# Moving two gate computations from the head of a query stage into the middle of the down stage before it

## The chip, the cores and the metric

The kernel runs on one core of one Trainium2 chip. The time is device microseconds of one execution, as the median over several runs. A core has engines that run side by side, each with its own in-order instruction queue: TensorE (PE, with its weight loads as PEld), VectorE (DVE), ScalarE (ACT), GpSimd (POOL) and SyncE (SP), which here issues most DMAs.

## The reference

Two branches work on the same input x (2048 rows of 1024 bf16 values) and are mixed by a gate, one number for each row:

```python
g = sigmoid((x * gate_w).sum(-1, keepdims=True))
a = attention(x, wqkv) @ wo      # 32 heads of 32, window of 8 keys at distance 2
b = (gelu(x @ w_gate) * (x @ w_up)) @ w_down     # 3584 wide
out = g * a + (1 - g) * b
```

Each query looks at the keys 0, 2, ... 14 rows back; keys ahead of the first row are masked.

## The kernel before, in words

The 2048 rows are cut into four **chunks** of 512. Chunks 0 and 1 form the first pair, 2 and 3 the second. For each pair the program makes queries, keys and values (`qkv_pair`, `first_pair`), then the GLU branch (`ffn`), and then for each chunk the **down stage** (`down`, `down_rest`), which multiplies the GLU result by w_down and the attention result by wo and adds both in the same PSUM banks. So TensorE's order is: query, key and value products of pair 0, `ffn` 0, down 0, query, key and value products of pair 1, some blocks of `ffn` 1, down 1, the rest of `ffn` 1, down 2, down 3.

All large products of a pair are made in a scheme of seven products where eight would be plain (Strassen's, in Winograd's form). It needs sums and differences of the operands, made on VectorE:

- **forms of x**: four operations in `x_forms` (L516, L518, L520, L521). L520 overwrites part of chunk 2's x, so it must come after the gate of that chunk has read x.
- **forms of the weights**: for the queries, keys and values eight operations on L709 for each (four forms in two halves, `qkv_forms`).
- **forms of the GLU result** for the down stage (L1266, `down_forms`).

The seven products of a down stage are numbered m = 0 to 6, each made for two halves g = 0, 1. Product 0 is in `begin`; products 1 to 6 run in `down_rest` in the order (1,0), (1,1), (2,0) ... (6,1). Each is 18 matmuls of 128x512 on line L1305: 14 with the GLU result (tile hT) and four with the attention result (tile qo). What each leaves: m = 2 a scaled copy m5d in the buffers with tag `m5`, m = 3 a copy u2d in those with tag `u2`; m = 4 adds its bank and m5d into an output tile (L1377 before the change), m = 5 its bank and u2d (L1383), m = 1 and m = 6 are scaled out by ScalarE (L1346). The output tiles are stored by GpSimd (L1338). In this text the "fifth product" is m = 4 and the "sixth" is m = 5.

The query products of the second pair begin in `first_pair` with line L592: for t = 0 to 3, a product over the first half of the contraction (four matmuls, and a seeding copy L604 by ScalarE), then the second half (L592 again, copied out by L625). Then come the products of the forms on L772, at first with tf (forms of x), and after the queries the rest in `qkv_pair`, where a bank with a product is copied or added out by L798, L808, L820, L830 and L858 (ScalarE) and by **L837** and **L847** (VectorE). A later product (T4 in `qkv_pair`) is accumulated in the bank which L837 has read, so TensorE waits for L837 there. The same part in `first_pair` is done by L657 and L667.

**The gate** of chunk c (`gate`): eight matmuls (L874) of gate_w with x into one PSUM bank, a 32x32 block transpose of it to a tile zt in SBUF by VectorE (L880), and a small copy zq of every 32nd column (L884). The bank is given back after L880. `gate_sum` later sums zq by a small matmul.

**Attention** of a chunk is VectorE work that goes on beside all stages: `scores` multiplies queries with shifted keys (L937) and adds up (L943); the sum is turned by a DMA transpose (L1006); L1014 to L1060 make the softmax; ScalarE spreads the weights (L1066); two DMA transposes of 256 KB each (**L1075**) turn them back; then L1084 multiplies with the values and L1094, L1098, L1102 add up. The first L1084 waits for both L1075.

**Who sets the order.** A planner (`Weave`) takes a number of streams (main, loads, scores, attention, forms and so on), estimates with costs that are written in the code when each next operation could start, and emits the earliest one, with a bias or a due time for some. The order in which it emits is fixed for each engine by manual dependencies. So where one step in `main` is moved, the planner may choose another order for the operations of other streams around it, on every engine. Once built, every engine's queue is in that order whatever the real times are.

Weights arrive in a **ring** of 20 slots of 256 KB (L352 for the query, key and value weights, L400 for `ffn`, L420 for down), loaded by SyncE in a fixed order; a load waits for its slot to be given back. L1075 and L1006 are issued by SyncE too and stand in the same queue. An L709 needs the loads of its weights; the first one waits for all eight loads of its matrix. Eight PSUM banks of 128x512 float32 are handed out by `bank_take`, the one that the planner thinks free the earliest first.

## Time and profile before

| what | value |
|---|---|
| median of 4 runs | 725.92 us (725.33 to 727.16) |
| the profiled execution's own time | 726.34 us |
| its span, first to last instruction | 724.6 us |
| granted TensorE clock, mean | 0.998 |
| TensorE busy in the span | 711.5 us |
| VectorE busy in the span | 610.1 us |
| first down stage (L1305), about | 250.9 to 307.8 us |
| gates of chunks 2 and 3 (L874) | 307.76 to 308.74 us |
| query products of the second pair (L592) | 308.74 to 321.1 us |
| key and value products (L772) | up to 388 us |

The profile is of one execution. Times are from the start of its span. A timeline's row has start, duration, engine, source line, operation, tiles written and read, and in brackets how long the engine was idle before it and what ended that. A row of windows has, for a stretch of time, the busy time of each engine with its instruction count, the granted TensorE clock as a share, the DMA engines' share and GB/s. Matmuls overlap, so one takes 0.379 us but they follow each other every 0.216 us. Rows of VectorE overlap a little too: an operation shown as 1.22 us lets the next one start after 1.13 to 1.14.

### The profile page before, as it was taken

To read this page: it belongs to the slowest core of one execution; us is meant where nothing else is said; L and a number is where in the kernel's file an instruction comes from. 1 tells how busy PE (TensorE), PEld (TensorE's weight loads), DVE (VectorE), ACT (ScalarE), POOL (GpSimd) and SP (SyncE) were. 2 spreads that over 40 slices of the span, in tenths; PEclk is the share of its full clock that TensorE was granted. 3 is DMA by queue.
4 is the path that set the end of the run, shared out by engine and by line. 5 is a ranking of instruction groups with operands and counts; after the bars stand their busy time and mean duration, and the time that the engine had idled before them with its cause. 6 is when DMAs were issued, how large, how long until landed. Compare 5 with 4: busy or idle time off the path is not lost.

```text
span 724.6 us, 9885 instructions
## 1 busy us (share of the span) xinstructions
PE 711.5 (98%) x3337; PEld 342.8 (47%) x3337; DVE 610.1 (84%) x862; ACT 323.8 (45%) x547; POOL 73.8 (10%) x130
## 2 busy tenths in 40 slices
PE   7999999999999999979999999999999999999997
PEld 4556544444444444446655444444444444444443
DVE  4989999999999999699779998799999997849300
ACT  3354585555585422144465413257556755310110
POOL 0021233343111000100000000100000000001000
PEclk9999999999999999999999999999999999999999
DMA  9943899996897799932468899997657755999992
GB/s 265 369 179 101 262 279 333 350 316 203 199 255 204 262 229 342 343 121 88 139 182 283 263 314 336 320 314 191 173 152 184 180 156 164 313 287 378 312 328 97
DMA packets 184179, 176.84 MB, mean 244 GB/s; under 512 B 58304, under 2 KB 140224, under 8 KB 184000
## 3 DMA queue, kind: packets, MB, share of 16 engines
q1 hardware_dynamic: 174512, 145.53, 68.4%
q0 software_dynamic: 9328, 30.42, 11.4%
q8 instruction: 26, 0.43, 0.2%
q10 hardware_dynamic: 288, 0.26, 0.1%
q14 instruction: 25, 0.20, 0.1%
HBM read 132.12 MB, written 31.46 MB: 226 GB/s over the span
## 4 chain that ended last, share of the span: by engine, by line
PE 94%; DMA 2%; DVE 2%; SPq 1%; issue 0%; ACT 0%; DVEq 0%
PE ps L1136 47%; PE ps L1305 29%; PE ps L772 18%; DMA ring<-in_A_wqkv_dram 2%; DVE ring L709 1%; PE ps L592 1%; SPq L357 1%; DMA hT<-in_A_wqkv_dram 1%; DVE zt L880 0%; SPq L428 0%; DVE tf L518 0%; DVE tf L521 0%; DVE lend L520 0%; DVE lend L837 0%; ACT ost L1346 0%
## 5 line engine op out<-in xcount | busy, mean ns | idle before, releaser
L1136 PEld LDWEIGHTS <-ring 128*128 128x128 bf16 x1568 | 153.3, 98 | 185.0 <-issue 0.5
L1136 PE MATMUL ps<-lend,ring 128*128 128x512 bf16 x896 | 212.6, 379 | 0.0
L1136 PE MATMUL ps<-tf,ring 128*128 128x512 bf16 x672 | 164.3, 379 | 0.0
L1305 PE MATMUL ps<-ring,hT 128*128 128x512 bf16 x708 | 160.6, 379 | 0.0
L1305 PEld LDWEIGHTS <-hT 128*128 128x128 bf16 x708 | 69.3, 98 | 83.5
L1084 DVE TENSOR_TENSOR xbuf<-xbuf,lend 128x2048 bf16<-128x2048 bf16 x64 | 77.6, 1218 | 14.4 <-DMA xbuf<-xbuf 14.3
L772 PEld LDWEIGHTS <-ring 128*128 128x128 bf16 x512 | 64.8, 127 | 48.7 <-issue 2.6
L937 DVE TENSOR_TENSOR xbuf<-qo,lend 128x2048 bf16<-128x2048 bf16 x64 | 77.3, 1218 | 2.7 <-ACT lend L830 2.6
L943 DVE TENSOR_TENSOR xbuf<-xbuf 128x2048 bf16<-128x2048 bf16 x56 | 68.2, 1218 | 0.2
L772 PE MATMUL ps<-tf,ring 128*128 128x512 bf16 x256 | 58.4, 379 | 2.4 <-DVE tf L516 0.9
L772 PE MATMUL ps<-lend,ring 128*128 128x512 bf16 x256 | 57.9, 379 | 0.0
L1346 ACT ACTIVATE ost<-ps,omg 128x512 bf16<-128x512 f32 x16 | 11.0, 687 | 99.6 <-PE ps L1305 99.6
L1212 ACT ACTIVATE gl<-ps 128x512 bf16<-128x512 f32 x56 | 33.5, 598 | 47.8 <-PE ps L1136 46.6
L1168 ACT COPY ps<-ps 128x512 f32<-128x512 f32 x56 | 32.1, 573 | 50.9 <-PE ps L1136 50.6
L1305 PE MATMUL ps<-ring,qo 128*128 128x512 bf16 x192 | 49.3, 379 | 0.0
L1338 POOL DMA_DIRECT2D out_dram<-ost x24 | 13.0, 541 | 335.7 <-ACT ost L1346 248.0
L505 POOL DMA_DIRECT2D fforms<-ring x56 | 30.8, 550 | 144.3 <-DVE ring L496 138.3
L1185 DVE TENSOR_TENSOR hT<-hT,gl 128x1024 bf16<-128x1024 bf16 x56 | 38.4, 686 | 8.3 <-ACT hT L1178 8.2
L1224 DVE TENSOR_TENSOR u<-ps,u 128x512 f32<-128x512 f32 x56 | 38.4, 686 | 3.2 <-PE ps L1136 2.3
L1228 ACT ACTIVATE gl<-u 128x512 bf16<-128x512 f32 x56 | 35.4, 633 | 9.9 <-DVE u L1224 9.5
L1220 ACT COPY u<-ps 128x512 f32<-128x512 f32 x56 | 32.8, 586 | 14.6 <-PE ps L1136 14.6
L1094 DVE TENSOR_TENSOR xbuf<-xbuf 128x2048 bf16<-128x2048 bf16 x32 | 39.0, 1219 | 0.1
(120 smaller groups left out, 671.3 us busy)
## 6 DMA issues: line engine op xcount, KB each, us to landing
ring<-dforms SPq DMA_DIRECT2D x112, 256.0 KB, 4.9
ring<-in_B_w_down_dram SPq DMA_DIRECT2D x84, 256.0 KB, 5.4
ring<-in_B_w_gate_dram SPq DMA_DIRECT2D x56, 256.0 KB, 5.3
fforms<-ring POOLq DMA_DIRECT2D x56, 256.0 KB, 5.1
ring<-fforms SPq DMA_DIRECT2D x56, 256.0 KB, 4.0
ring<-in_B_w_up_dram SPq DMA_DIRECT2D x42, 256.0 KB, 4.8
ring<-in_A_wqkv_dram SPq DMA_DIRECT2D x32, 256.0 KB, 4.5
ring<-oforms SPq DMA_DIRECT2D x32, 256.0 KB, 5.4
```

Of the source, the lines that this page charges most:

```text
L772: nc.tensor.matmul(banks[bk][:], lhsT=lhsT, rhs=rhs[:, kt, :], start=(start and kt == 0), stop=(kt == KH - 1), skip_group_check=True)
L937: V(out=w3(box[t]), in0=q_b, in1=k_w, op=ALU.mult)
L943: V(out=w3(box[0]), in0=w3(box[0]), in1=w3(box[t]), op=ALU.add)
L1084: return dve(tt(n), taking(("p", t), lambda: V(out=w3(box["p", t]), in0=w3(box["ab"]), in1=v_w, op=ALU.mult)), [("qkv", c, 2, t), abo] + ( ...
L1094: V(out=p0.rearrange("p (u n) -> p u n", u=2), in0=lo, in1=hi, op=ALU.add)
L1136: nc.tensor.matmul(banks[bk][:], lhsT=wv[:, k, fl * P:(fl + 1) * P], rhs=rhs[:, k, :], start=(start and k == 0), stop=(k == KH - 1), skip_ ...
L1185: yield dve(tt(2 * SC), lambda hv=hv, gv=gv: nc.vector.tensor_tensor(out=hv, in0=hv, in1=gv, op=ALU.mult), [e, ev[f, "g1"], ev[f, "g2"]], ...
L1212: nc.scalar.activation(out=gl[f][:, r1 * SC:(r1 + 1) * SC], in_=banks[A[f]][:], func=ACT.Gelu_apprx_tanh)
L1220: nc.scalar.copy(out=u2[f][:], in_=banks[Bk[f]][:])
L1224: e = dve(tt(SC, True), lambda f=f: nc.vector.tensor_tensor(out=u2[f][:], in0=banks[Dk[f]][:], in1=u2[f][:], op=ALU.add), [o, ev[f, "u2"]])
L1228: ev[f, "g2"] = act(0.54, lambda f=f: nc.scalar.activation(out=gl[f][:, r2 * SC:(r2 + 1) * SC], in_=u2[f][:], func=ACT.Gelu_apprx_tanh), [ ...
L1305: nc.tensor.matmul(banks[bk][:], lhsT=l, rhs=wv[:, i, :], start=(start and k == 0), stop=(q == last and i == 1), skip_group_check=True)
```

## The change

`main` made the gates of chunks 2 and 3 after the first down stage, just ahead of the second pair's query products. Now `down_rest` of chunk 0 makes both just ahead of its product (5, 0), the sixth; the tile zt of those two gates comes from the buffers with tag `m5` rather than `u2`. Nothing else in the text of the program differs.

```diff
-        zt = work.tile([P, SC], F32, tag="u2", bufs=2, name="zt")
+        zt = work.tile([P, SC], F32, tag="m5" if c > 1 else "u2", bufs=2, name="zt")
...
         for m, g in steps:
+            if (m, g) == (5, 0) and c == 0:
+                yield from gate(2)
+                yield from gate(3)
...
         yield from parts[2]
         yield from halo(2)
-        yield from gate(2)
-        yield from gate(3)
         yield from qkv_pair(2, [0])
```

In the built program the lines behind the insertion are three higher, so L1377 becomes L1380 and L1383 becomes L1386. The planner also orders some other operations anew. The listing of the two built programs shows, from the fifth product on:

- VectorE before: L1377, L937, L943, L937, L1383, L943, L943, L937, L1383, L943, six L709, L520, L521, L880, L709, L884, L880, L709, L884, L1084, L1084, L1094, L1084, ...
- VectorE after: L1380, L520, L521, L880, L884, L880, L884, L937, L1386, L943, L1386, L1084, L1084, L1094, eight L709, L1084, L1098, L943, L1084, ...; and two L937 and two L943 stand just ahead of the first L837 of the key and value products.
- SyncE before: two L352, L1075, six L352, L1075, fourteen L352. After: two L352, L1075, L1075, twenty L352.
- GpSimd: the same order. ScalarE: the same kinds of operations in nearly the same order, on other banks.

## The prediction

> **What bounds the kernel now.** I read the page's first and fourth parts, then the chain in order of time, then the timelines of the stage that the change touches, from 290 to 350 us.

> ```profile
> PE 711.5 (98%) x3337; PEld 342.8 (47%) x3337; DVE 610.1 (84%) x862; ACT 323.8 (45%) x547; POOL 73.8 (10%) x130
> ...
> PE 94%; DMA 2%; DVE 2%; SPq 1%; issue 0%; ACT 0%; DVEq 0%
> ```

> TensorE is the bound, so only holes in its row are worth time. After the start there are two. The large one is in TensorE's timeline, at the head of the second query products (L592):

> ```profile
> 308.74 2.81 PE L592 MATMUL ps<-lend,ring 128*128 128x512 bf16 x12
> 315.39 5.89 PE L592 MATMUL ps<-lend,ring 128*128 128x512 bf16 x20 [3.84 <-DVE zt L880]
> 321.12 1.24 PE L772 MATMUL ps<-tf,ring 128*128 128x512 bf16 x5
> ```

> Twelve matmuls are done, and the thirteenth waits 3.84 us for the gate's transpose (L880), which reads the bank that it is to write. The other 20 then take 5.73 us to the next product, though at 0.216 each (6.90 us for the 32 from 321.12 to 328.02) they need 4.32. The windows say why (start:end, then TensorE busy; the last three columns are granted clock, DMA share, GB/s):

> ```profile
> 311.60:314.90 3.30, 0.00 (x0) 0.00 (x0) 3.30 (x5) 0.57 (x1) 0.00 (x0) 1.00 0.00 0
> 315.00:318.20 3.20, 2.81 (x7) 1.14 (x7) 3.20 (x7) 0.57 (x1) 0.00 (x0) 0.50 0.00 0
> 318.40:321.00 2.60, 2.60 (x14) 1.74 (x13) 2.57 (x4) 1.72 (x3) 0.00 (x0) 1.00 0.96 329
> ```

> After the idle stretch the clock is 0.50. So the hole costs 3.84 + (5.73 - 4.32) = 5.25 us. VectorE's timeline says why the transpose was late:

> ```profile
> 301.26 1.22 DVE L943 TENSOR_TENSOR xbuf<-xbuf 128x2048 bf16<-128x2048 bf16 x1
> 308.61 3.83 DVE L709 TENSOR_TENSOR ring<-ring 128x1024 bf16<-128x1024 bf16 x6 [6.14 <-DMA ring<-in_A_wqkv_dram]
> 312.35 1.22 DVE L520 TENSOR_TENSOR lend<-lend 128x2048 bf16<-128x2048 bf16 x1
> 313.49 1.22 DVE L521 TENSOR_TENSOR tf<-lend,tf 128x2048 bf16<-128x2048 bf16 x1
> 314.62 0.71 DVE L880 STREAM_TRANSPOSE zt<-ps 128x512 f32<-128x512 f32 x1
> ```

> It idles 6.14 us until the query weights land, then makes six weight forms (L709) and two forms of x, and only then transposes. SyncE's queue shows those loads around two DMA transposes (L1075):

> ```profile
> 296.80 0.92 SPq L352 DMA_DIRECT2D ring<-in_A_wqkv_dram  x2
> 298.01 1.47 SPq L1075 DMA_TRANSPOSE xbuf<-xbuf  x1
> 299.58 3.31 SPq L352 DMA_DIRECT2D ring<-in_A_wqkv_dram  x6
> 303.16 1.23 SPq L1075 DMA_TRANSPOSE xbuf<-xbuf  x1
> ```

> [...] halved from about 314.9, 3.3 us after the last matmul.[...] a wait holds all behind it, as L880 was held behind L709 here.[...] the second transpose, issued last, moves last.[...]

> ```profile
> 301.50:302.50 1.00, 1.00 (x7) 0.41 (x6) 0.97 (x1) 0.00 (x0) 0.54 (x1) 1.00 0.24 28
> 302.50:303.50 1.00, 1.00 (x6) 0.48 (x5) 0.00 (x0) 0.00 (x0) 0.00 (x0) 1.00 0.77 197
> 303.50:307.50 4.00, 4.00 (x21) 1.76 (x18) 0.00 (x0) 0.69 (x1) 0.54 (x1) 1.00 1.05 385
> 307.50:308.50 1.00, 1.00 (x18) 0.33 (x16) 0.00 (x0) 0.58 (x1) 0.00 (x0) 1.00 1.15 301
> ```

> **TensorE's part.** The two gates' 16 matmuls take 0.98 us (start 307.76, next product 308.74). They go ahead of the sixth product, to 292.2; the four products behind them run 0.98 later, and the query products start at 308.74 as before. Net zero. Their banks are then read long before the query products want them, so the wait for L880 is gone: 32 matmuls from 308.74 end at 308.74 + 32 x 0.217 = 315.7, not 321.12. Removed: 5.4 us. Next late are the forms: the first is wanted at 315.7.

> **The buffer tag.** zt moves to m5's pair, whose readers are the fifth product's two adds (L1377), ahead of the transposes on VectorE anyway: nothing. In u2's pair it would have waited for the sixth product's adds (L1383).

> **VectorE's part.** By the build's listing, L520, L521, two transposes and two copies move up behind the second L1377, to 293.0 (3.70 us: 312.35 to 317.19 less two L709). They displace five score operations (two L937, three L943, 1.135 each, 5.68 us) to behind the forms: one in between, four just ahead of L837. And two L1084 and an L1094 (3.53 us, 317.19 to 320.72), which wait for both DMA transposes, now stand **ahead of the forms**, so a late transpose holds them too.

> **SyncE's and Pool's parts.** The second transpose is issued right behind the first, ahead of six weight loads. Pool's order stays; two output stores come 0.98 later, nobody waits. The transpose's cost is not shown in this place. Lower bound: its own 0.26 MB at 301 GB/s, 0.9 us. Upper: the first one's slot; between the loads ahead (low by 300.5) and those behind (303.5) lie 3.0 us with a hole at 28 GB/s. I take 1.2: the hole is at the first one, which stays where it is. The last load landed at 302.56 + 5.83 = 308.39, so now at 309.6; SyncE's issue (about 303.6 for the last) is not the limit. The second transpose lands by about 305.3 (the first did at 298.01 + 6.0 = 304.0), the three operations behind it end at 305.3 + 3.5 = 308.8, hidden under the loads. L709 starts 0.2 after the last landing, at **309.8**.

> **The new wait.** Behind that VectorE's queue is full. In the trace of before, L709's start (308.61) to the end of the L1102 ahead of L837 (346.2) is 37.6 us, of which 1.4 idle: 36.2 busy. Now it is 36.2 - 3.70 - 3.53 + 5.68 = 34.65, with 0.2 of small waits 34.85; so L837 starts at 344.65. The product that is added onto its result's bank (the L772 product that begins at 348.75 in the trace) can start 0.74 later (as at 372.97 and 373.71): 345.4. Unhindered, TensorE would be there at 348.75 - 5.4 = 343.35. So it waits about 2.0 us for L837: below 3.3, so the clock holds. Forms and banks on the way are in time by the same sum; the nearest is a bank given by L667 at 333.1, wanted at 333.9.

> **What comes after.** The later steps hang on TensorE's place: the second hole (0.63 at 373, for L837 behind a VectorE wait of 3.80 for a parking DMA) follows a copy out of the products, and moves along. The turn of the scores (L1006, 344.24) now waits for the last L943, to 344.6: same place, hidden, since what follows it has 2 us of room. I count nothing more.

> **Sum.** 5.4 - 2.05 = 348.75 - 345.4 = 3.3 us off the span: 724.6 to 721.3. The profiled execution took 726.34, 1.74 outside its span; 723.0 on that footing. The median of before, 725.92, is 0.42 lower than that execution: **722.6**.

> **Rivals.**
> - Transposes dear. The second one's slot is like the first's, 3.0 instead of 1.2: L709 at 311.6, L837 later by 1.8, gain 1.5: **724.4**; with the delayed loads a little worse. For it: the hole of 28 GB/s follows a transpose behind loads. Against: the second one shows none. I put the case at 724.7. Chance 0.15.
> - VectorE keeps up. If the score operations cost TensorE nothing (L837 in time by slack I didn't see), the whole 5.3 stays: **720.6**. For it: 3 to 4 us of idle VectorE at 302 to 306. Against: its order is fixed, and the five operations stand ahead of L837. Chance 0.13.
> - Slower: VectorE is stopped at L1084, ahead of the forms. L709 starts 3.7 after the second landing L; the gain is gone when L709 starts 3.3 later than 309.8, that is L = 309.4, and it is slower by over 0.2% from 310.9. At L = 311.4 it is **727.9**. For it: issued at 303.16, that transpose landed at 309.7. Against: it is now issued at 299.6, and the longest of 16 took 7.1 from issue to landing. Chance 0.06.
> - The move isn't made, or another stall takes all: 725.9. The listing shows the gate matmuls ahead of the sixth product. Chance 0.02.

> The sum itself has 0.64, with its own range 721.5 to 724.0 (0.9 to 3.0 for the transpose, and half a microsecond either way for the queue).

> **Chances.** About 0.2% (1.45 us) can be told from no change. Faster: 0.64 + 0.13 = 0.77. Within: 0.15 + 0.02 = 0.17. Slower: 0.06. The range goes from the full gain to the dear transpose, 720.5 to 725.0, and leaves out 0.08 and some ends.

> **What would show it.** Right: no wait for L880 and no clock of 0.50 near 315; L592 in one run from 308.7 to 315.7; two L1075 in a row at 298 and 299.6; L709 from 309.8; a TensorE wait of about 2 us for L837 near 343. Wrong: L709 after 311.5 (transposes), a TensorE wait elsewhere, or no wait at L837.

## The result and the profile after

The changed kernel takes **722.76 us** as the median of 43 runs (721.78 to 726.21), against 725.68 for the kernel before (64 runs, 722.87 to 728.98): a ratio of 0.9967, 95% interval 0.9959 to 0.9975. The prediction was 722.6. The profiled execution of after took 722.93 with a span of 721.1; its page opens and its chain ends so:

```profile
PE 711.0 (99%) x3337; PEld 343.4 (48%) x3337; DVE 609.8 (85%) x862; ACT 323.6 (45%) x547; POOL 73.8 (10%) x130
...
PE 96%; DVE 1%; SPq 1%; DMA 1%; issue 0%; ACT 0%; DVEq 0%
```

The instruction counts are the same, the work on every engine is the same within 0.5 us, and TensorE's share of the chain is up from 94% to 96%: what went is waiting, and the stretch at half clock behind it. TensorE's timeline, at the places that the prediction named:

```profile
309.67 7.07 PE L592 MATMUL ps<-lend,ring 128*128 128x512 bf16 x32
316.58 7.07 PE L772 MATMUL ps<-tf,ring 128*128 128x512 bf16 x32
...
345.50 1.89 PE L772 MATMUL ps<-tf,ring 128*128 128x512 bf16 x8 [1.13 <-DVE lend L837]
...
370.27 1.89 PE L772 MATMUL ps<-tf,ring 128*128 128x512 bf16 x8 [0.43 <-DVE lend L837]
```

The 32 products of L592 are one run of 6.91 us, where before they took 12.38 with the hole; the wait for L880 is gone. A new wait of 1.13 us stands at L837, as forecast. The clock stays up (windows: the granted clock is the third column from the right):

```profile
310.00:320.00 10.00, 10.00 (x48) 6.13 (x47) 9.84 (x14) 7.26 (x14) 0.54 (x1) 1.00 0.42 138
...
345.00:346.00 1.00, 0.50 (x3) 0.36 (x3) 1.00 (x3) 0.00 (x0) 0.00 (x0) 1.00 0.00 0
```

VectorE's timeline shows what L837 waited behind: eight weight forms that begin when the last query weight lands, and, just ahead of it, the four score operations that the planner had put off:

```profile
309.63 5.22 DVE L709 TENSOR_TENSOR ring<-ring 128x1024 bf16<-128x1024 bf16 x8 [1.32 <-DMA ring<-in_A_wqkv_dram]
...
340.10 2.35 DVE L937 TENSOR_TENSOR xbuf<-qo,lend 128x2048 bf16<-128x2048 bf16 x2
342.37 2.48 DVE L943 TENSOR_TENSOR xbuf<-xbuf 128x2048 bf16<-128x2048 bf16 x2
344.76 1.28 DVE L837 TENSOR_TENSOR lend<-ps,m5q 128x512 bf16<-128x512 f32 x2
```

On SyncE's queue the two L1075 do stand together, but the second keeps the queue for 4.00 us, so that the six loads behind begin at 301.9:

```profile
295.92 1.39 SPq L1075 DMA_TRANSPOSE xbuf<-xbuf  x1
297.81 4.00 SPq L1075 DMA_TRANSPOSE xbuf<-xbuf  x1
301.91 1.00 SPq L352 DMA_DIRECT2D ring<-in_A_wqkv_dram  x2
```

Where the time went can be read from the starts of the same products in both timelines (before less after): L592 starts 0.93 us *later* after (308.74, 309.67; that lag is there 21 us into the span, at 20.65 against 21.57 for the same L772 product, ahead of anything that the change touches), L592 itself gives 12.38 - 6.91 = +5.47, the stretch from there to the product behind L837 gives 27.63 - 28.92 = -1.29, the stretch on to the second hole 24.96 - 24.77 = +0.19, and the rest is equal. Sum 3.44; the last products start at 719.82 and 716.37, 3.45 apart.

### The profile page after: what moved, and what is told of

The parts are those of the page before. It is cut to its first block, busy times and chain, and to the rows that moved or that the text cites. A ratio compares the mean times of both kernels' runs of the same rounds, so it can differ in the third digit from the quotient of the medians.

```text
span 721.1 us, 9892 instructions
## 1 busy us (share of the span) xinstructions
PE 711.0 (99%) x3337; PEld 343.4 (48%) x3337; DVE 609.8 (85%) x862; ACT 323.6 (45%) x547; POOL 73.8 (10%) x130
## 4 chain that ended last, share of the span: by engine, by line
PE 96%; DVE 1%; SPq 1%; DMA 1%; issue 0%; ACT 0%; DVEq 0%
PE ps L1136 47%; PE ps L1305 30%; PE ps L772 18%; PE ps L592 1%; SPq L357 1%; DMA hT<-in_A_wqkv_dram 1%; DVE ring L709 0%; SPq L428 0%; DVE lend L837 0%; DVE tf L518 0%; DVE zt L880 0%; PE ps L874 0%; ACT ost L1346 0%; DVE hT L709 0%; PE ps L898 0%
## 5 line engine op out<-in xcount | busy, mean ns | idle before, releaser
L1084 DVE TENSOR_TENSOR xbuf<-xbuf,lend 128x2048 bf16<-128x2048 bf16 x64 | 77.7, 1219 | 16.7 <-DMA xbuf<-xbuf 16.6
L772 PEld LDWEIGHTS <-ring 128*128 128x128 bf16 x512 | 64.7, 127 | 50.1 <-issue 3.8
L937 DVE TENSOR_TENSOR xbuf<-qo,lend 128x2048 bf16<-128x2048 bf16 x64 | 77.0, 1218 | 2.3 <-ACT lend L830 2.3
L943 DVE TENSOR_TENSOR xbuf<-xbuf 128x2048 bf16<-128x2048 bf16 x56 | 68.2, 1218 | 0.2
L772 PE MATMUL ps<-tf,ring 128*128 128x512 bf16 x256 | 58.4, 379 | 3.5 <-DVE lend L837 1.6
L772 PE MATMUL ps<-lend,ring 128*128 128x512 bf16 x256 | 57.9, 379 | 0.0
L1228 ACT ACTIVATE gl<-u 128x512 bf16<-128x512 f32 x56 | 35.4, 633 | 12.8 <-DVE u L1224 12.3
L1094 DVE TENSOR_TENSOR xbuf<-xbuf 128x2048 bf16<-128x2048 bf16 x32 | 39.0, 1219 | 0.1
```

The lines of the kernel that those rows point to most:

```text
L772: nc.tensor.matmul(banks[bk][:], lhsT=lhsT, rhs=rhs[:, kt, :], start=(start and kt == 0), stop=(kt == KH - 1), skip_group_check=True)
L937: V(out=w3(box[t]), in0=q_b, in1=k_w, op=ALU.mult)
L943: V(out=w3(box[0]), in0=w3(box[0]), in1=w3(box[t]), op=ALU.add)
L1084: return dve(tt(n), taking(("p", t), lambda: V(out=w3(box["p", t]), in0=w3(box["ab"]), in1=v_w, op=ALU.mult)), [("qkv", c, 2, t), abo] + ( ...
L1094: V(out=p0.rearrange("p (u n) -> p u n", u=2), in0=lo, in1=hi, op=ALU.add)
L1228: ev[f, "g2"] = act(0.54, lambda f=f: nc.scalar.activation(out=gl[f][:, r2 * SC:(r2 + 1) * SC], in_=u2[f][:], func=ACT.Gelu_apprx_tanh), [ ...
```

## The experiments

In some of these kernels the lines are moved down: in run 3 L938 and L945 are L937 and L943, in run 6 L1087 is L1084. All ratios are to runs of the kernel before on the same chip.

**1. The tag alone.** Gates at the old place, zt in the m5 pair.

```diff
-        zt = work.tile([P, SC], F32, tag="u2", bufs=2, name="zt")
+        zt = work.tile([P, SC], F32, tag="m5" if c > 1 else "u2", bufs=2, name="zt")
```

> The kernel before with the buffer tag of zt alone changed to m5 for chunks 2 and 3; the gates stay in the old place, and every engine's order is that of before. My theory: the tag costs and gains nothing, since the last readers of the m5 pair are done some 15 us earlier: about 725.7, ratio 1.000 within 0.002, the wait of 3.84 us for L880 and the clock of 0.50 behind it unchanged. Rival (the pair is still held when the transpose is to write it): L880 later, the hole longer, over 726.5.

725.75 us, ratio 1.0002 (0.9983 to 1.002): the tag does nothing that can be measured. But its profile, with the order of before, isn't that of before. TensorE's timeline and windows:

```profile
308.77 2.81 PE L592 MATMUL ps<-lend,ring 128*128 128x512 bf16 x12
313.98 6.16 PE L592 MATMUL ps<-lend,ring 128*128 128x512 bf16 x20 [2.40 <-DVE zt L880]
319.98 7.07 PE L772 MATMUL ps<-tf,ring 128*128 128x512 bf16 x32
```

```profile
314.00:315.00 1.00, 1.00 (x5) 0.71 (x5) 1.00 (x3) 0.00 (x0) 0.00 (x0) 1.00 0.00 0
315.00:316.00 1.00, 1.00 (x5) 0.48 (x3) 1.00 (x4) 0.57 (x1) 0.00 (x0) 0.60 0.00 0
316.00:317.00 1.00, 1.00 (x3) 0.33 (x2) 1.00 (x2) 0.57 (x1) 0.00 (x0) 0.50 0.21 27
```

The hole is 2.40 us, not 3.84 (the first L709 began at 307.20, not 308.61), and the clock halves all the same, 1.2 us after TensorE is at work again. The prediction's "below 3.3, so the clock holds" was no sound reason. This opened two questions: how long is the hole in other executions, and what halves the clock.

**2. The old place, with the transpose first.** One bias in the kernel before.

```diff
-        e = dve(0.63, lambda: nc.vector.transpose(out=zt[:], in_=banks[i][:]), [o], bias=-2.0 if c < 2 else None)
+        e = dve(0.63, lambda: nc.vector.transpose(out=zt[:], in_=banks[i][:]), [o], bias=-2.0)
```

> The kernel before with one bias changed: the gates stay at the head of the query products, but VectorE takes the first L880 ahead of L520 and L521, so it starts about 2.27 us earlier (312.35 rather than 314.62), behind the same six L709. My theory, with the clock as a term of its own: the hole shrinks from 3.84 to about 1.6 us, the clock stays at 1.00, and the 20 matmuls behind it take 4.5 us rather than 5.9. TensorE is then 2.27 + 1.41 = 3.7 us earlier, until VectorE's chain stops it: L837 starts at about 345.0, the product behind it at 345.75 rather than at 345.07, a wait of some 0.7 us. Net 3.0 us less: about 722.7. Rival (the slow matmuls come from something else at this place, a contention with the transposes and weight forms, so they stay slow): 5.9 us for the 20 matmuls and only 2.3 us less in the span, about 723.4.

722.55 us, ratio 0.9968 (0.9954 to 0.9981). TensorE's and VectorE's timelines:

```profile
309.03 7.13 PE L592 MATMUL ps<-lend,ring 128*128 128x512 bf16 x32
```

```profile
306.79 3.83 DVE L709 TENSOR_TENSOR ring<-ring 128x1024 bf16<-128x1024 bf16 x6 [4.02 <-DMA ring<-in_A_wqkv_dram]
310.53 0.71 DVE L880 STREAM_TRANSPOSE zt<-ps 128x512 f32<-128x512 f32 x1
```

In this execution the loads landed early, L880 was ahead of TensorE, and no hole was left, so nothing here tells the clock's term; the rival (contention keeps the products slow) is out, as the 32 ran in 7.13 us (7.07 in the changed kernel) with the clock at 1.00, beside L520, L521 and the forms. What it does show: the gain of the change can be had without moving a matmul. What cost time was where L880 stood on VectorE.

**3. The four score operations cut short.** The changed kernel; the last two L937 and L943 of chunk 1's second half work on 16 of 256 rows each, so that most of these scores are left out.

```diff
-                        V(out=w3(box[0]), in0=w3(box[0]), in1=w3(box[t]), op=ALU.add)
+                        n_ = 16 if h == 3 and t in TORD[-2:] else AC
+                        V(out=w3(box[0])[:, :, 0:n_], in0=w3(box[0])[:, :, 0:n_], in1=w3(box[t])[:, :, 0:n_], op=ALU.add)
```

(the L937 likewise)

> The changed kernel, same order on every engine, with the last two L937 and the last two L943 of chunk 1's second half cut to 16 of 256 rows each (that part of the scores is left out), so that the four operations just ahead of the first L837 take some 0.6 us rather than 4.66. My theory, the displaced score operations hold L837 and it holds TensorE: L837 no longer late, the wait of 1.13 us at 345 gone, the product there follows its predecessor at once; 1.1 to 2.0 us less than the changed kernel, about 721.3. Rival (VectorE is not what sets TensorE's place there; a copy by ScalarE or a load is next): another wait of about the same length in the same place, about 722.7.

721.22 us, ratio 0.9948 (0.993 to 0.9967), 1.5 less than the changed kernel's median. VectorE's timeline, and then TensorE's:

```profile
339.66 0.36 DVE L938 TENSOR_TENSOR xbuf<-qo,lend 128x128 bf16<-128x128 bf16 x2
339.93 0.48 DVE L945 TENSOR_TENSOR xbuf<-xbuf 128x128 bf16<-128x128 bf16 x2
341.32 0.69 DVE L837 TENSOR_TENSOR lend<-ps,m5q 128x512 bf16<-128x512 f32 x1 [0.90 <-PE ps L772]
```

```profile
343.64 1.89 PE L772 MATMUL ps<-tf,ring 128*128 128x512 bf16 x8
```

Now L837 waits for TensorE and not TensorE for L837. The chain on VectorE from L709 to L837 was the bound, as the prediction had it; the rival is out.

**4. The score operations kept in their place.** The gates' matmuls stay moved; their transposes go behind the first add of the sixth product, and the planner may emit L520 and L521 only after the last score operation. SyncE's order is that of the changed kernel.

```diff
+            if (m, g) == (5, 1) and c == 0:
+                yield from late[2]
+                yield from late[3]
...
-            yield dve(t, lambda b12=b12, b22=b22: V(out=b12, in0=b22, in1=b12, op=ALU.subtract), [("z", cb)], key=("xf", sup, 3), bias=-1.0 if sup else -0.3)
+            yield dve(t, lambda b12=b12, b22=b22: V(out=b12, in0=b22, in1=b12, op=ALU.subtract), [("z", cb)] + ([("qk", 3)] if sup else []), key=("xf", sup, 3), bias=-1.0 if sup else -0.3)
```

(late holds the part of the gate behind its matmuls; L521 gets the same dependence)

> The changed kernel with VectorE's order mended: gate matmuls at the same place, but the score operations stay where they were before the change, the gates' transposes go behind the first add of the sixth product, L520 and L521 behind the last score operation, and the first L1084 behind the eight L709. SyncE's order is that of the changed kernel. My theory: L709 starts with the last weight load as in the changed kernel, about 309.6; VectorE's chain to L837 is 36.2 - 3.7 = 32.5 us long, so L837 starts at about 342, ahead of TensorE: no wait near 345, the whole gain of 5.3 us kept, 720.6 to 721.4. Rival (the gain is limited by the DMA transposes ahead of the weight loads, not by the scores): a wait of 1 us or more near 345 stays, about 722.7.

721.66 us, ratio 0.9951 (0.9935 to 0.9966). VectorE's and TensorE's timelines:

```profile
310.72 5.21 DVE L709 TENSOR_TENSOR ring<-ring 128x1024 bf16<-128x1024 bf16 x8 [3.73 <-DMA ring<-in_A_wqkv_dram]
...
343.44 1.28 DVE L837 TENSOR_TENSOR lend<-ps,m5q 128x512 bf16<-128x512 f32 x2
```

```profile
344.18 1.89 PE L772 MATMUL ps<-tf,ring 128*128 128x512 bf16 x8 [0.33 <-DVE lend L837]
```

The chain is 343.44 - 310.72 = 32.7 us (32.5 expected, 35.1 in the changed kernel), and even with the weights a microsecond later than there TensorE waits only 0.33. No wait was expected, and the median lies 0.3 above the range given, as the weights came at 310.72 and not at 309.6. So what the score operations add to the wait is the planner's choice, not a price of the move.

**5. The transposes apart.** The changed kernel with the second L1075 planned behind the eight query loads.

```diff
-            o = turn(n // 2, taking("ab", back) if i == 0 else back, [es[i]], pre=xb_pre() if i == 0 else None)
+            o = turn(n // 2, taking("ab", back) if i == 0 else back, [es[i]] + ([("wqkv", 2, 0, 7)] if h == 2 and i else []), pre=xb_pre() if i == 0 else None)
```

> The changed kernel with the second L1075 of chunk 1's first half planned behind all eight query weight loads, so SyncE has the order of before: two L352, L1075, six L352, L1075. With it the planner puts the score operations back ahead of the forms and the L1084 behind them. My theory now: the second transpose ahead of six loads costs these about 2.3 us rather than the 1.2 that I took (from the first L352 to the first L709 there passed 11.8, 13.3 and 12.7 us in three runs with it behind, 15.4, 14.7 and 14.7 with it ahead). So L709 starts 12.6 us after the first L352, about 307; L837 is ready by about 340, no wait near 345: 720.6 to 721.4, about 0.3 less than with the scores kept and the transposes ahead. Rival (the price of the pair is small, and the difference is the moment at which the loads begin in each run): 14 to 15 us from the first L352 to the first L709 here too.

721.28 us, ratio 0.9942 (0.9928 to 0.9956). SyncE's queue and VectorE's first form:

```profile
296.81 1.26 SPq L1075 DMA_TRANSPOSE xbuf<-xbuf  x1
298.37 2.86 SPq L352 DMA_DIRECT2D ring<-in_A_wqkv_dram  x6
301.60 1.23 SPq L1075 DMA_TRANSPOSE xbuf<-xbuf  x1
```

```profile
307.01 0.69 DVE L709 TENSOR_TENSOR ring<-ring 128x1024 bf16<-128x1024 bf16 x1 [0.90 <-DMA ring<-in_A_wqkv_dram]
```

Apart, each transpose holds SyncE for some 1.25 us; together, the second held it for 3.2 to 4.0 (the changed kernel twice, runs 3, 4, 6 and 8). The first L709 came at 307.01, as expected, 11.4 us after the first L352 (12.6 expected), and no wait near 345 is left. That wait went for two reasons at once: the planner also put the score operations back, ahead of the forms and one behind the first form, so the 1.5 us gained on the changed kernel can't be split between them. The landing of the loads can be read by itself. A steadier mark than the first L352 is the first L1075. From its issue to the first L709 passed, in us: with the second behind the loads 10.60 (before), 11.63, 11.03 (runs 1 and 2), 10.20 (here), 10.22 and 11.13 (runs 7 and 9), mean 10.8; with it ahead 13.71 (after), 13.07, 12.56 (runs 3 and 4) and 12.83 (run 10), mean 13.0. So the second transpose's place costs the loads **2.2 us**, or 2.8 if only kernels with the gates moved are compared (10.2 in runs 5 and 7). No run has both transposes ahead of the loads with something between them, so it isn't shown whether it matters that they stand in a row, or only that both are ahead.

**6. A third transpose.** The changed kernel with the second L1075 issued once more.

```diff
+        if h == 2:
+            o = turn(n // 2, back, [es[1]])
+            yield o
```

> The changed kernel with the second L1075 issued once more behind itself (the same data, so one DMA transpose of 256 KB more ahead of the last six query weight loads). My theory: each transpose there costs about 2.3 us, so L709 starts some 17 us after the first L352, L837 is 2.3 later, the wait near 345 becomes 3.4 us, and the clock may halve behind it (1.4 us more): 725.1 without, 726.5 with that. Rival of the prediction (a transpose costs its own bytes, 0.9 to 1.2 us): 724.0, a wait of 2.2 us, clock at 1.00.

728.71 us, ratio 1.0046 (1.0029 to 1.0063): slower than either guess. SyncE's queue (the second row is the third transpose by itself), and TensorE's timeline:

```profile
297.15 8.17 SPq L1075 DMA_TRANSPOSE xbuf<-xbuf  x3
...
304.09 1.23 SPq L1075 DMA_TRANSPOSE xbuf<-xbuf  x1
305.42 18.34 SPq L352 DMA_DIRECT2D ring<-in_A_wqkv_dram  x14
```

```profile
332.97 2.99 PE L772 MATMUL ps<-tf,ring 128*128 128x512 bf16 x9 [2.30 <-DVE qo L657]
...
350.68 3.20 PE L772 MATMUL ps<-tf,ring 128*128 128x512 bf16 x8 [2.05 <-DVE lend L837]
```

L709 began at 313.81, 16.7 us after the first L1075, 3.6 more than with two. That isn't the price of a transpose by itself, for the third one writes the tile of the second again, and SyncE first stood for the second's landing:

```profile
SPq L1075 <- DMA xbuf<-xbuf: 2.4, 1, 2.4
```

Once it began, it held the queue for only 1.23 us. VectorE is then late at L657 too, which I hadn't counted, and the clock halves behind both waits. The prediction's slower case had VectorE held at L1084 by the transpose; here the first two L1087 (L1084 elsewhere) were done by 309.7, and L709 then stood 4.13 us for its loads. The end is the same, all of the gain lost, but the way to it leads through SyncE's queue. Windows of 0.2 us at the edges of the slow stretches:

```profile
334.00:334.20 0.20, 0.20 (x2) 0.14 (x1) 0.20 (x2) 0.17 (x1) 0.00 (x0) 0.57 0.00 0
337.40:337.60 0.20, 0.20 (x2) 0.14 (x1) 0.20 (x1) 0.20 (x1) 0.00 (x0) 0.90 0.00 0
351.00:351.20 0.20, 0.20 (x3) 0.13 (x2) 0.20 (x2) 0.00 (x0) 0.00 (x0) 0.74 0.00 0
354.40:354.60 0.20, 0.20 (x2) 0.07 (x1) 0.00 (x0) 0.10 (x1) 0.00 (x0) 0.73 0.00 0
```

The third number from the right is the granted clock. A share of 0.57 between 1.00 and 0.50 puts the edge 0.03 us into the window, and so on: down at 334.03, up at 337.44, down at 351.10, up at 354.51. Each slow stretch is 3.41 us long, and the two begin 17.07 us = 5 x 3.41 apart.

**7. The best of these, and L837 first at the second hole.** Run 5's kernel, with the first forms of the next down stage planned 2 us later.

```diff
-            return dve(tt((NTH if part else FH) * P), fn, deps, key=(name, c, g, part))
+            return dve(tt((NTH if part else FH) * P), fn, deps, key=(name, c, g, part), lag=2.0 if c == 1 and name == "S1" and part == 0 else 0.0)
```

> The kernel of the run with the transposes apart, and beside that the planner told that the first L1266 of the next down stage start 2 us later, so that the two L837 near 372 stand ahead of it on VectorE and not behind its wait for the parking DMA. My theory: the last hole of TensorE after the start, 0.3 to 0.5 us near 370, goes, and nothing else: 0.3 to 0.5 less than with the transposes apart, about 720.6. Rival (L1266, now behind, holds the next down stage or L847): the same or slower.

**720.08 us**, ratio 0.9928 (0.9913 to 0.9944): the fastest, 2.7 less than the change alone. From 285 us on TensorE waits for nothing. VectorE's timeline:

```profile
365.55 0.69 DVE L837 TENSOR_TENSOR lend<-ps,m5q 128x512 bf16<-128x512 f32 x1 [4.01 <-PE ps L772]
366.15 1.08 DVE L1266 TENSOR_TENSOR hT<-hT 128x1792 bf16<-128x1792 bf16 x1
```

L837 now goes ahead of L1266. The gain over run 5 is 1.2, more than the 0.3 to 0.5 expected: in run 5 TensorE waited for L837 once more, 0.22 us at 382, which goes as well. By the starts of the same products in the two profiles the two waits had cost 0.6 and 0.4 us; 0.2 of the medians' difference is not accounted for.

**8. The old place, both transposes behind the loads.**

```diff
-            o = turn(n // 2, taking("ab", back) if i == 0 else back, [es[i]], pre=xb_pre() if i == 0 else None)
+            o = turn(n // 2, taking("ab", back) if i == 0 else back, [es[i]] + ([("wqkv", 2, 0, 7)] if h == 2 else []), pre=xb_pre() if i == 0 else None)
```

> The kernel before, gates at their old place, with both L1075 of chunk 1's first half planned behind all eight query weight loads; seven L709, L520 and L521 still stand ahead of the first L880. My theory: the hole of before is set by the landing of these loads, so with no transpose among them L709 starts about 2.3 us earlier (10.3 us after the first L352), the hole shrinks from 2.4 to 3.8 us to about 0.5 and the clock stays at 1.00: 721.0 to 722.0, as good as the change without moving the gates. Rival (the order on VectorE alone makes the hole, or the loads wait for their ring slots): the hole stays over 2 us, about 725.

724.18 us, ratio 0.9993 (0.9978 to 1.0009): no gain to be measured; what I expected did not come. The first L709 came at 306.65, 12.3 us after the first L352, no earlier than with a transpose among the loads. SyncE's waits say why: the eight L352 stood 3.5 us for earlier loads (tiles dforms and oforms) to land. A single transpose among the loads (1.26 us of SyncE in run 5) may hide in that, which is my estimate of why only the second one ahead of them costs anything; no run shows it. TensorE's timeline and windows are worth a look:

```profile
314.03 4.48 PE L592 MATMUL ps<-lend,ring 128*128 128x512 bf16 x20 [2.31 <-DVE zt L880]
```

```profile
314.00:315.00 1.00, 0.97 (x5) 0.69 (x5) 1.00 (x3) 0.00 (x0) 0.00 (x0) 1.00 0.00 0
315.00:316.00 1.00, 1.00 (x7) 0.65 (x6) 1.00 (x2) 0.62 (x2) 0.00 (x0) 1.00 0.37 53
```

A hole of 2.31 us, and the clock stays at 1.00; in run 1 a hole of 2.40 halved it.

**9 and 10. Both kernels once more, unchanged.**

> The kernel before, unchanged, for a second look at its hole. My theory: the first look was one with a late landing of the query weights (first L709 at 308.6 in it, at 306.7 to 307.2 in three runs with a transpose order like it), so the hole at L592 here is nearer 2.3 us than 3.84, and whether the clock halves behind it differs from execution to execution: with it about 725.5, without it about 724. Rival (the 3.84 us and the clock of 0.50 are what this order always gives, and the tag of zt took 1.4 us off the hole): 3.8 us again, about 726.

> The changed kernel, unchanged, for a second look at its wait. My theory: the first L709 14.5 to 15.5 us after the first L352 again, and the wait for L837 near 345 follows its place: a landing earlier by a microsecond takes the wait away (about 722), one later by a microsecond makes it 2 us and may halve the clock (about 724.5). Rival (the wait is fixed by the order): 1.1 us again wherever L709 starts.

Before took 724.58. TensorE's timeline:

```profile
309.39 2.81 PE L592 MATMUL ps<-lend,ring 128*128 128x512 bf16 x12
315.11 4.48 PE L592 MATMUL ps<-lend,ring 128*128 128x512 bf16 x20 [2.91 <-DVE zt L880]
319.43 7.07 PE L772 MATMUL ps<-tf,ring 128*128 128x512 bf16 x32
```

A hole of 2.91 us with the clock up. After took 722.91:

```profile
345.56 1.89 PE L772 MATMUL ps<-tf,ring 128*128 128x512 bf16 x8 [1.34 <-DVE lend L837]
```

The wait is 1.34 with L709 at 309.70, 13.9 us after the first L352 (14.5 to 15.5 expected), and L592 at 309.52. L709 lay within 0.1 us of its place in the other execution, so whether the wait follows it in single executions of this kernel isn't told by the pair; runs 4 and 6 tell it for other kernels. The sum for this pair, by the same starts: -0.13 (L592), +3.13 (10.04 to 6.91), -1.51, +0.17, that is 1.66 us; the last products are 1.66 apart.

## Why the prediction was right, step by step

- **The hole at L592 goes**: right in kind and place. 5.4 us was its size in the one execution shown. The order of before gave three sizes, by L592's whole length less 6.91: 5.47, 4.30 (run 1) and 3.13 (run 9), mean 4.3, as the loads land at other moments and the clock halves or not. I took one execution's hole for the typical one, and then set the sum on the median's footing.
- **The clock's term, 1.41**: real, but not in every execution. One slow stretch of 3.41 us takes 0.0024 from the mean granted clock of the whole span. Of 53 executions of before that were run beside the experiments, 31 had a mean below 0.999, with a median of 726.1, and 22 had at least that, with 724.1. Of 44 of after 7 were below (724.9) and 37 not (722.6). So the change takes off about 1.5 us where the clock didn't halve, and makes the halving rarer. "Below 3.3, so the clock holds" failed as a reason: waits of 2.05, 2.30 and 2.40 us were followed by the half clock, waits of 2.31 and 2.91 weren't, nor were 1.13 and 1.34. The 3.3 was the time from the last matmul to the one halving in the trace of before, taken for the length that a hole must have; in run 6 a hole of 2.05 was enough. The last section has my estimate of what told them apart.
- **The gates' matmuls and the tag at nothing**: right. The sixteen take 0.98 us at the new place, the four products behind them keep their rate, and run 1 has the tag.
- **L709 at 309.8**: it came at 309.63 and 309.70, by luck: two errors cancel. The second transpose costs 2.2 to 2.8 us and not 1.2 (the loads stand behind a queue that is held for 4 us, which I had put aside as "not the limit"), and in the profile of before the first L1075 was issued at 298.01, where the nine other executions with one of these two orders had it from 295.57 to 298.16, 296.6 in the mean. The price is nearer the 3.0 of the dear transposes' rival than my 1.2; that rival's end (724.7) was off since it was set on the same late landing.
- **L837 at 344.65, the product at 345.4**: 344.76 and 345.50. The chain from L709 to L837 took 35.1 us, and 34.85 was forecast. Runs 3 and 4 show the mechanism: without the displaced operations the wait goes, or all but 0.33 of it.
- **A wait of 2.0 us**: 1.13 and 1.34. TensorE came later than I had it, 309.67 and 309.52 for L592 rather than 308.74, and found VectorE less late. The rival in which VectorE keeps up is out by this wait, and the slower one by VectorE's timeline: the first L1084 began at 304.69, so the second transpose had landed by then (305.3 forecast), and the three operations were done ahead of the last load.
- **What comes after**: the second hole moved along, with 0.43 us and 0.39 for 0.63 and 0.55. Run 7 shows that it costs more than its length, 0.6 us for a wait of 0.44.

Why the total held: in part by luck. With the means of these executions the gain is 4.3 - 1.4 + 0.2 = 3.1 us, the medians give 2.9, and the prediction had 3.3. The hole was taken 1.1 too large and the wait behind it 0.6 too large, and in a difference these errors offset each other. That both hang on the same landing, so that a late one lengthens both, would be a reason, but the two pairs of executions don't show it: the longer hole (5.47) went with the smaller loss behind it (1.29), the shorter one (3.13) with the larger (1.51). What was lost of the full gain went into a chain on VectorE that the planner had lengthened, and into loads that it had put behind a second transpose; the move asked for neither.

## What to carry to other kernels

When a planner emits the order, price a moved step by what else changes place: here a transpose that had come to stand ahead of six loads made these 2.2 to 2.8 us late, four score operations that had come to stand ahead of L837 made TensorE wait 1.13, one bias (run 2) bought as much as the move, and two small constraints on the planner (run 7) brought nearly as much again. Take the size of a hole from several executions when it ends on a load's landing. And set no value on a hole's length as such for the clock: here waits of 2.05, 2.30 and 2.40 us were followed by the half clock (behind it the 20 products took 6.00 us in run 1, against 4.32 in run 9), waits of 2.31 and 2.91 were not, and the kernel before showed both in its executions.

## What the runs showed of the hardware

The grid also fits the two holes that left the clock up. At the end of the span, behind the last product, the clock falls once more, and in before this edge fits the grid of its slow stretch. The windows there, of before and of runs 8 and 9:

```profile
724.40:724.50 0.10, 0.00 (x0) 0.00 (x0) 0.00 (x0) 0.00 (x0) 0.00 (x0) 0.87 0.00 0
721.80:722.00 0.20, 0.00 (x0) 0.00 (x0) 0.00 (x0) 0.00 (x0) 0.00 (x0) 0.68 0.00 0
722.60:722.80 0.20, 0.00 (x0) 0.00 (x0) 0.00 (x0) 0.00 (x0) 0.00 (x0) 0.81 0.00 0
```

Read as above, the edges are at 724.47, 721.87 and 722.72. In before, 724.47 - 314.88 = 409.59 us is 120 stretches of 3.413 (119 would make it 3.44, 121 3.39). Runs 8 and 9 have no slow stretch to read the grid from; by estimate, the same 409.59 counted back from the edge at the end puts one at 312.28 in run 8 and at 313.13 in run 9, and each cuts the hole: 2.31 us (from 311.71) into 0.57 and 1.75, and 2.91 us (from 312.20) into 0.93 and 1.98. The stretches that were followed by the half clock held 2.05 and 2.30 (run 6), 2.19 (run 1) and 3.3 us (before) of idle TensorE. My estimate from these five traces is that the idle time within one stretch of the grid told the two cases apart: by the profile's ends of matmuls the clock stayed up with 1.98 of 3.41 us idle (run 9) and halved with 2.05 (run 6). The holes of 2.31 and 2.91 us would then have left it up since an edge divided each into two parts of at most 1.98.

**A DMA transpose held its queue for microseconds.** In the stage of the change the second of a pair held SyncE for 3.2 to 4.0 us, a single one for 1.2 to 1.5, and a plain load of 256 KB for 0.3 to 0.5. Standing in a row is not what decides it everywhere. Two lines of SyncE's queue in before, the first for a transpose 19 us behind the one ahead of it, the other for one 1.7 us behind:

```profile
453.27 3.34 SPq L1075 DMA_TRANSPOSE xbuf<-xbuf  x1
508.02 1.23 SPq L1075 DMA_TRANSPOSE xbuf<-xbuf  x1
```

What decides the hold is not shown. In this case transposes and loads differ: the window of a transpose in before's profile has 301 GB/s and that of the loads 385, and a second transpose ahead of the loads brought these in 2.2 to 2.8 us later, where by estimate 256 KB at those 385 GB/s take some 0.7.
